# Attention mix on one core: one gate pass for all tokens, a landing rule for VectorE in the kernel's own scheduler, and a new table of its settings

## The chip, the core and the metric

The kernel runs on one core of a Trainium2 chip. The metric is the device time of one execution in microseconds, as a median of several runs. Times inside an execution come from one run taken with the hardware profiler; they count from its first instruction.

## What is computed

Two attentions over the same 2048 tokens of width 640, 32 heads of 20, mixed by a gate for each token:

```python
g = sigmoid((x * gate_w).sum(-1, keepdims=True))
# A: full softmax attention (every query with all 2048 keys)
scores = einsum("bhqd,bhkd->bhqk", q, k) * scale ; p = softmax(scores) ; o = p @ v ; a = o @ A_wo
# B: each query with 8 keys, 2 positions apart (idx = pos - 2 * w, masked below 0)
logits = einsum("bhsd,bhswd->bhsw", q, kg) * scale ; o = softmax(logits) @ vg ; b = o @ B_wo
return g * a + (1 - g) * b
```

## The kernel before, in words

The work of A sets the shape. Queries are taken in four chunks of 512 tokens and heads in eight groups of four: a *group* is one chunk with four heads, 32 groups in all (the last one is done in two halves of 256 tokens). The first 16 groups belong to chunks 0 and 1, the next eight to chunk 2, the last eight to chunk 3. Inside a group, a *unit* is one head with 128 keys: a matmul of contraction 32 that makes 128 x 512 scores in PSUM, then an exponential, then a product with the values that adds up in one bank, `obank`.

Scores go through two PSUM tiles, `score0` and `score1`, in turn. Each has three banks. A *tile* of work is two units or three: `qk(s)` (line 1690) issues its score matmuls (line 1708; row tiling, up to four heads at once), `exp(s)` (line 1728) lets ScalarE do the exponential of 1024 or 1536 columns into `ebuf` (line 1731), and `pv` (line 1743) issues the value products (line 1783; column tiling). Score tile s+2 needs the bank that exponential s reads.

Part of the units go to VectorE instead. Such a *ride* is one more score matmul in a tile, put into the third bank or into `side0`. VectorE turns it into an approximate exponential in integer arithmetic, by the scaled score put into the bits of a bf16 (line 1721, written as `uD`). Four rides make a quad; the quad's value product is done four times with weighted values (`vS`, made by GpSimd at line 893), and between these VectorE adds a constant to the bits (line 902). `wanted` and `next_tile` (lines 1562 and 1634) decide which units ride.

Everything else shares three *side banks*: `side0` and the third banks of the two score tiles. Python generators describe this work piece by piece: `gen_kd`, `gen_qd`, `gen_v` (the projections of A; a matmul group at line 606, then a VectorE copy out of the bank, lines 648, 721, 791), `gen_gate` (line 813), `gen_norm` (line 836: transpose of `obank`, reciprocal of the sums at line 844, scaling by `gA` and by the reciprocals on GpSimd at lines 850 and 858, transpose back at line 874, and transfers to `oTd`), `gen_bproj` and `gen_b` (all of B: copies at line 958, products at lines 974 and 1072, its own softmax and gate, with `tB` by a tanh at line 1048 and a reciprocal at line 1051), and `gen_fold` and `gen_prefold` (the output projections).

The order on each engine is made when the kernel is built. A scheduler written in the kernel keeps an estimated clock for each engine and appends instructions to five in-order lists. The loop over tiles lays `qk`, `exp` and `pv`; what room TensorE has left until the exponential ends is given to the generators (`run_side`, line 1343). A generator stops at a request such as `("pe", cost, ready)`, `("bank", need)`, `("act", ready)` or `("dve",)`, and `step` (line 1285) says whether it may go on now. For VectorE the test before was only how far that engine's own list had already been filled, and a ready time where the request named one:

```python
        elif req[0] == "dve":
            if not force and (sch.avail["dve"] > now + (req[1] if len(req) > 1 else DVE_AHEAD) or
                              len(req) > 2 and req[2] > max(now, sch.avail["dve"])):
                return False
```

`run_dve` (line 1351) fills VectorE's list in the same way ahead of a ride's conversion. `PLAN` is a table of 22 settings of this scheduler (slacks, priorities, how many units ride, when filler matmuls are laid), with new values from certain tiles on. Fillers (line 1804) are matmuls whose result nobody reads.

The gate in A's output: four matmuls of 32 columns for each of 5 parts of the width repeat the sum over all 128 partitions for one chunk of 512 tokens (line 606), a transpose (line 825) brings tokens to partitions, a tanh (line 828) and one VectorE operation (line 830) make `gA`. This is done once a chunk: for chunks 0 and 1 when group 1 begins, for chunk 2 and 3 shortly before their groups.

Of the kernel before, what the change touches and what calls it, by code (L numbers as in the profile page):

```python
# [10 lines left out]
ALU = mybir.AluOpType  # L11
# [9 lines left out]
CN = D // P  # L21
# [34 lines left out]
    0: ((0.3, 0.64), 0.32, 2.5, 2.5, 0.49, -1.3, -0.1, 11.8, 7.0, 7.2, 0.5, 0.47, 4.4, 4.0, -0.23, 0.75, 2, 0.0, 0.5, 4.0, 3.0, 1.0),  # L56
    10: ((0.28, 0.73), 0.32, 6.6, 2.5, 0.49, -0.79, -0.1, 11.8, 6.2, 5.51, 0.49, 0.47, 5.1, 4.63, -0.1, 0.75, 2, -1.5, 0.32, 4.0, 3.0, 1.0),
    30: ((0.28, 0.73), 0.32, 6.6, 2.5, 0.58, -0.79, -0.68, 11.8, 6.2, 5.51, 0.49, 0.47, 5.1, 4.63, -0.1, 0.72, 2, 0, 0.25, 4.0, 3.0, 1.0),
    40: ((0.28, 0.73), 0.32, 6.6, 2.5, 0.58, -0.79, -0.68, 11.8, 6.2, 5.51, 0.49, 0.47, 5.1, 4.63, 0.03, 0.74, 2, 0, 0.25, 4.0, 2.0, 0.0),
    50: ((0.28, 0.73), 0.32, 6.6, 2.5, 0.58, -0.79, -0.68, 12.65, 6.2, 5.51, 0.49, 0.47, 5.1, 4.63, -0.11, 0.74, 2, 0, 0.25, 4.0, 2.0, 0.0),  # L60
    60: ((0.28, 0.73), 0.37, 1.0, 2.5, 0.59, -0.79, -0.44, 11.8, 1.0, 6.14, 0.49, 0.47, 5.1, 4.63, -0.1, 0.72, 2, -3, 0.25, 4.0, 3.0, 1.0),
    70: ((0.28, 0.73), 0.37, 1.0, 2.5, 0.59, -0.79, -0.44, 11.8, 1.0, 6.14, 0.49, 0.52, 5.1, 4.63, -0.1, 0.72, 2, -3, 0.21, 4.0, 3.0, 1.0),
    80: ((0.28, 0.73), 0.32, 6.6, 5.5, 0.54, -0.74, -0.68, 12.65, 6.2, 6.19, 0.49, 0.47, 5.1, 5.79, -0.09, 0.66, 2, 0, 0.25, 4.0, 3.0, 0.0),
    90: ((0.28, 0.73), 0.13, 6.6, 5.5, 0.54, -0.74, -0.68, 12.65, 6.2, 6.19, 0.49, 0.47, 5.1, 5.79, -0.09, 0.66, 2, 0, 0.43, 4.0, 3.0, 0.0),
    100: ((0.28, 0.73), 0.13, 6.6, 6.6, 0.54, -0.74, -0.68, 12.65, 6.2, 6.19, 0.49, 0.47, 5.1, 5.79, -0.23, 0.63, 2, 0, 0.43, 4.0, 3.0, 0.0),
    110: ((0.28, 0.73), 0.36, 6.6, 6.6, 0.7, -0.74, -0.68, 12.65, 6.2, 6.19, 0.49, 0.47, 5.1, 5.79, -0.09, 0.66, 2, -3, 0.31, 4.0, 4.0, 0.0),
    120: ((0.28, 0.73), 0.36, 6.6, 6.6, 0.7, -0.48, -0.68, 12.65, 6.2, 6.19, 0.49, 0.47, 5.1, 5.65, -0.09, 0.66, 2, -3, 0.31, 4.0, 2.0, 0.0),
    140: ((0.28, 0.73), 0.36, 6.6, 6.6, 0.7, -0.48, -0.68, 12.87, 6.2, 5.74, 0.49, 0.47, 5.1, 5.65, -0.09, 0.66, 2, -3, 0.3, 4.0, 3.0, 0.0),
    150: ((0.28, 0.73), 0.45, 6.6, 2.5, 0.7, -0.48, -0.68, 12.87, 6.2, 5.74, 0.49, 0.47, 5.1, 6.51, -0.09, 0.72, 2, -3, 0.3, 4.0, 3.0, 0.0),
    160: ((0.28, 0.73), 0.5, 1.0, 2.5, 0.71, -0.48, -0.27, 12.87, 7.0, 5.74, 0.49, 0.47, 5.1, 7, -0.09, 0.72, 2, -3, 0.3, 4.0, 3.0, 0.0),  # L70
    170: ((0.24, 0.73), 0.46, 1.0, 6.6, 0.71, -0.89, 0.05, 12.87, 7.0, 5.74, 0.42, 0.47, 4.74, 7, -0.09, 0.72, 2, -3, 0.39, 4.0, 3.0, 0.0),
    180: ((0.24, 0.73), 0.46, 1.0, 6.6, 0.71, -0.89, 0.05, 12.87, 7.0, 5.74, 0.42, 0.47, 4.74, 7, -0.09, 0.72, 1, -3, 0.39, 4.0, 3.0, 0.0),
    190: ((0.28, 0.73), 0.42, 6.6, 6.6, 0.7, -0.74, -0.86, 12.65, 6.2, 6.19, 0.49, 0.38, 5.1, 5.79, -0.09, 0.66, 2, -3, 0.25, 4.0, 2.0, 0.0),
    200: ((0.28, 0.73), 0.42, 6.6, 6.6, 0.7, -0.61, -1.0, 10.61, 6.2, 7.31, 0.53, 0.38, 4.59, 5.79, 0.11, 0.66, 1, -3, 0.25, 4.0, 2.0, 0.0),
    220: ((0.28, 0.73), 0.31, 6.6, 6.6, 0.7, -0.61, -1.0, 9.36, 6.2, 7.31, 0.53, 0.38, 4.59, 5.79, 0.11, 0.66, 1, -3, 0.25, 4.0, 2.0, 0.0),
    230: ((0.25, 0.73), 0.33, 1.0, 1.0, 0.49, -0.79, -0.39, 11.8, 6.2, 5.77, 0.28, 0.47, 4.42, 4.63, -0.1, 0.73, 2, -3, 0.38, 4.0, 3.0, 0.0),
    240: ((0.25, 0.73), 0.33, 1.0, 1.0, 0.49, -0.79, -0.39, 11.8, 6.2, 5.77, 0.28, 0.45, 4.42, 4.63, -0.1, 0.73, 2, -3, 0.38, 4.0, 3.0, 0.0),
    250: ((0.28, 0.73), 0.5, 1.0, 5.5, 0.71, -0.48, -0.27, 12.87, 7.0, 5.74, 0.49, 0.65, 5.1, 7, -0.14, 0.72, 2, -3, 0.3, 4.0, 2.0, 0.0),
    260: ((0.28, 0.73), 0.5, 1.0, 5.5, 0.9, -0.48, -0.27, 12.87, 7.0, 5.74, 0.49, 0.65, 5.1, 7, -0.14, 0.72, 2, -3, 0.3, 4.0, 3.0, 0.0),
    270: ((0.28, 0.73), 0.5, 1.0, 1.0, 0.9, -0.48, -0.27, 12.87, 7.0, 6.71, 0.49, 0.65, 5.1, 7, -0.31, 0.72, 2, -3, 0.3, 4.0, 3.0, 0.0),  # L80
    280: ((0.28, 0.73), 0.59, 1.0, 1.0, 0.9, -0.48, -0.27, 12.87, 7.0, 6.71, 0.49, 0.69, 5.1, 7, -0.31, 0.72, 2, -3, 0.3, 4.0, 3.0, 0.0),
    290: ((0.28, 0.73), 0.31, 6.6, 2.5, 0.54, -0.74, -0.68, 11.34, 6.2, 8.37, 0.49, 0.47, 5.1, 5.79, -0.09, 0.74, 2, 0, 0.25, 4.0, 3.0, 0.0),
    300: ((0.28, 0.73), 0.31, 6.6, 2.5, 0.54, -0.74, -0.68, 11.34, 1.0, 8.37, 0.49, 0.32, 5.1, 5.79, -0.16, 0.74, 2, 0, 0.25, 4.0, 3.0, 0.0),
    310: ((0.28, 0.73), 0.31, 6.6, 2.5, 0.54, -0.74, -0.68, 11.34, 1.0, 8.37, 0.49, 0.1, 5.1, 5.79, -0.16, 0.74, 2, 0, 0.25, 4.0, 3.0, 0.0),
    320: ((0.38, 0.78), 0.22, 1.0, 6.6, 0.87, -0.76, -0.56, 12.65, 6.2, 6.19, 0.62, 0.38, 5.94, 6.4, -0.12, 0.73, 2, 0, 0.18, 4.0, 4.0, 0.0),
    330: ((0.38, 0.78), 0.22, 1.0, 6.6, 0.87, -0.76, -0.56, 12.65, 7.0, 6.19, 0.62, 0.38, 5.94, 5.7, -0.12, 0.73, 2, 1, 0.32, 4.0, 4.0, 0.0),
    340: ((0.38, 0.78), -0.02, 2.5, 6.6, 0.54, -0.76, -0.56, 12.65, 7.0, 6.19, 0.62, 0.38, 5.94, 5.7, 0.03, 0.73, 2, 1, 0.4, 4.0, 4.0, 0.0),
    350: ((0.28, 0.69), 0.29, 6.6, 6.6, 0.7, -0.48, -0.73, 12.65, 6.2, 4.72, 0.64, 0.47, 6.28, 6.04, -0.19, 0.66, 2, -3, 0.49, 4.0, 3.0, 0.0),
    360: ((0.28, 0.73), 0.32, 6.6, 2.5, 0.49, -0.79, -0.2, 11.8, 6.2, 7.02, 0.49, 0.47, 5.94, 5.65, -0.1, 0.73, 1, 0, 0.32, 4.0, 3.0, 1.0),
    370: ((0.28, 0.73), 0.32, 6.6, 2.5, 0.49, -0.79, -0.2, 11.8, 7.0, 7.91, 0.49, 0.47, 5.89, 5.65, -0.1, 0.67, 1, 0, 0.32, 4.0, 3.0, 1.0),  # L90
    390: ((0.28, 0.73), 0.21, 6.6, 5.5, 1.02, -0.48, -0.27, 12.69, 7.0, 5.74, 0.49, 0.65, 4.72, 7, -0.24, 0.75, 2, -3, 0.13, 4.0, 3.0, 1.0),
    400: ((0.28, 0.73), 0.21, 6.6, 1.0, 1.02, -0.48, -0.33, 12.76, 7.0, 5.74, 0.49, 0.77, 4.04, 7, -0.24, 0.75, 2, -3, 0.13, 4.0, 2.0, 1.0),
    410: ((0.28, 0.73), 0.21, 6.6, 1.0, 1.02, -0.48, -0.23, 12.76, 7.0, 5.74, 0.49, 0.77, 4.04, 7, -0.24, 0.75, 2, -3, 0.0, 4.0, 2.0, 1.0),
    420: ((0.28, 0.79), 0.21, 6.6, 5.5, 1.02, -0.48, -0.23, 12.76, 7.0, 5.39, 0.49, 0.77, 4.84, 7, -0.24, 0.7, 2, -3, 0.0, 4.0, 2.0, 1.0),
    430: ((0.28, 0.79), 0.21, 6.6, 5.5, 1.02, -0.48, -0.23, 9.83, 7.0, 5.39, 0.49, 0.77, 5.77, 7, -0.24, 0.73, 2, -3, 0.0, 4.0, 2.0, 1.0),
    450: ((0.28, 0.79), 0.21, 6.6, 5.5, 1.02, -0.48, -0.23, 9.83, 7.0, 5.39, 0.49, 0.77, 5.77, 7, -0.15, 0.73, 2, -3, 0.2, 4.0, 2.0, 1.0),
    470: ((0.28, 0.79), 0.21, 6.6, 5.5, 1.02, -0.67, -0.23, 9.83, 7.0, 5.39, 0.49, 0.77, 5.77, 7, -0.15, 0.73, 2, -3, 0.2, 4.0, 2.0, 1.0),
    490: ((0.28, 0.79), 0.21, 6.6, 1.0, 1.02, -0.89, -0.16, 9.83, 7.0, 5.39, 0.49, 0.58, 5.77, 7, -0.19, 0.73, 2, -3, 0.2, 4.0, 2.0, 1.0),
    500: ((0.28, 0.79), 0.21, 2.5, 1.0, 1.02, -0.89, -0.16, 9.55, 7.0, 5.39, 0.49, 0.58, 5.77, 7, -0.19, 0.73, 2, -3, 0.2, 4.0, 2.0, 1.0),
    510: ((0.28, 0.78), 0.32, 6.6, 6.6, 0.59, -0.74, -0.68, 12.65, 6.2, 6.19, 0.49, 0.38, 4.6, 5.79, -0.09, 0.68, 2, -3, 0.18, 4.0, 1.0, 1.0),  # L100
    520: ((0.33, 0.78), 0.32, 6.6, 6.6, 0.59, -0.95, -0.68, 12.65, 6.2, 6.19, 0.45, 0.38, 4.6, 5.79, -0.09, 0.68, 2, -3, 0.18, 4.0, 3.0, 1.0),
    530: ((0.28, 0.71), 0.21, 6.6, 5.5, 1.02, -0.48, -0.27, 12.69, 7.0, 5.74, 0.49, 0.71, 4.72, 6.53, -0.24, 0.75, 2, 0, 0.13, 4.0, 3.0, 1.0),
    540: ((0.28, 0.71), 0.21, 5.5, 1.0, 1.02, -0.48, -0.27, 12.37, 4.5, 5.74, 0.55, 0.71, 4.72, 6.53, -0.07, 0.75, 2, 0, 0.13, 4.0, 3.0, 1.0),
# [239 lines left out]
def _build(ctx, nc, A_x, A_wqkv, A_wo, B_wqkv, B_wo, gate_w, out):  # L343
# [469 lines left out]
    def gen_gate(qc):  # L813
        while qc > 1 and not all(done.get(("norm", POS[qc - 2, q])) for q in range(NQ)):
            yield ("cond",)
        while qc == 1 and not done.get(("gate", 0)) or qc > 1 and ulock[1]:
            yield ("cond",)
# [1163 lines left out]
```

## Time and profile before

| | before |
|---|---|
| runs | 802.10, 802.82, 803.96 us; median 802.82 |
| profiled execution | 802.35 us, span 800.5 us |
| ScalarE's first and last exponential start | 19.34 and 791.69 us |
| exponentials of 1024 / 1536 / 512 columns | 555 / 187 / 1 |
| rides converted by VectorE (line 1721) | 313 from score banks + 63 from `side0` |
| granted TensorE clock | 1.000 |

A line of the groups reads: source line, engine, operation, written tile, read tile and shapes, count, then busy time and mean duration in ns, then the engine's idle time ahead of these instructions and who ended it. A line of the waits reads: who waited, at which line, for whom; total us, how often, the longest. "issue" is idle time that the profile puts down to nothing. In the table by stretches every engine has its busy time and its count of instructions; then come the granted clock, the share of the DMA engines and GB/s. Engines overlap successive instructions, so durations of one engine may sum to more than the time that passes.

### The profile page before, as it was taken

What the parts mean: (1) busy time and instruction counts of PE and PEld (TensorE: products, weight loads), DVE (VectorE), ACT (ScalarE), POOL (GpSimd) and SP (SyncE); (2) the same over time, 40 slices, a digit from 0 to 9 for tenths busy, and PEclk for the clock granted to TensorE, in tenths of its full rate; (3) what the DMA queues carried; (4) which work ended last, traced back from release to release, by engine and by line L of the source; (5) the groups of instructions that cost most, each with busy time, mean ns of one, the idle gap of its engine ahead of it and who ended that gap; (6) DMA issues with size and microseconds to landing.
All of it is one profiled execution on the core that took longest, in us unless ns stands there. A gap on an engine that the chain in (4) does not pass through costs nothing.

```text
span 800.5 us, 29678 instructions
## 1 busy us (share of the span) xinstructions
PE 769.4 (96%) x12489; PEld 283.6 (35%) x12489; DVE 713.4 (89%) x1286; ACT 780.3 (97%) x777; POOL 144.8 (18%) x243
## 2 busy tenths in 40 slices
PE   8999989999999999999999999999999999899998
PEld 5333222233333343423343333333332333333243
DVE  6678889999888999898989999989999989899985
ACT  4999999999999999999999999999999999999996
POOL 5105111115411211111111011121011110211120
PEclk9999999999999999999999999999999999999999
DMA  9120101012012300300131130030220021103001
GB/s 304 53 50 7 29 16 34 23 36 70 22 35 49 67 20 19 77 12 22 35 90 22 28 85 14 22 91 23 57 48 10 17 64 44 32 6 73 10 11 35
DMA packets 59448, 35.27 MB, mean 44 GB/s; under 512 B 25252, under 2 KB 58116, under 8 KB 59316
## 3 DMA queue, kind: packets, MB, share of 16 engines
q1 hardware_dynamic: 59172, 33.21, 16.7%
q8 instruction: 99, 1.62, 0.8%
q14 instruction: 33, 0.27, 0.1%
q10 hardware_dynamic: 144, 0.16, 0.1%
HBM read 11.45 MB, written 2.62 MB: 18 GB/s over the span
## 4 chain that ended last, share of the span: by engine, by line
ACT 41%; PE 38%; issue 15%; DVE 4%; DMA 1%; SPq 0%; ACTq 0%
ACT ebuf L1731 41%; PE score L1708 13%; PE obank L1783 10%; PE side L606 7%; PE score L606 5%; DVE uD L1721 1%; DMA oB<-in_A_x_dram 1%; DVE uD L902 1%; PE score L990 0%; DVE kmd L651 0%; DVE qkvB L648 0%; ACT eB L1021 0%; PE score L1380 0%; PE obank L1804 0%; PE side L1804 0%
## 5 line engine op out<-in xcount | busy, mean ns | idle before, releaser
L1731 ACT ACTIVATE ebuf<-score 128x1024 bf16<-128x1024 f32 (+1 forms) x743 | 768.3, 1191 | 2.7 <-PE score L1708 1.7
L1708 PE MATMUL score<-qT,kT 32*128 32x512 bf16 (+1 forms) x2044 | 297.9, 378 | 22.4 <-ACT ebuf L1731 15.4
L1721 DVE TENSOR_SCALAR uD<-score 128x512 int16<-128x512 f32 x313 | 209.3, 681 | 25.6 <-PE score L1708 24.7
L902 DVE TENSOR_SCALAR uD<-uD 128x2048 int16<-128x2048 int16 x282 | 191.6, 698 | 6.3 <-PE obank L1783 5.7
L1708 PEld LDWEIGHTS score<-qT,kT 32*128 32x128 bf16 x2044 | 73.1, 91 | 265.5 <-ACT ebuf L1731 192.0
L1783 PE MATMUL obank<-ebuf,vA 128*21 128x512 bf16 (+1 forms) x1724 | 165.4, 380 | 0.6 <-DVE uD L902 0.4
L893 POOL TENSOR_TENSOR vS<-vA,vw 128x252 bf16<-128x252 bf16 x94 | 58.5, 622 | 455.0 <-DVE uD L902 239.4
L1783 PE MATMUL obank<-uD,vS 128*21 128x512 bf16 (+1 forms) x1128 | 98.2, 376 | 0.0
L606 PE MATMUL side<-xT,kvw 128*32 128x256 bf16 (+1 forms) x1960 | 82.6, 285 | 0.4 <-DVE uD L1721 0.3
L1783 PEld LDWEIGHTS obank<-ebuf,vA 128*21 128x21 bf16 x1724 | 41.2, 89 | 99.0 <-issue 77.0
L606 PEld LDWEIGHTS side<-xT,kvw 128*32 128x32 bf16 x1960 | 47.1, 96 | 26.4 <-issue 12.5
L974 DVE TENSOR_TENSOR stage<-qkvB 128x1280 bf16<-128x1280 bf16 x64 | 50.5, 813 | 0.0
L1072 DVE TENSOR_TENSOR stage<-stage,eB 128x1280 bf16<-128x1280 bf16 x64 | 50.3, 814 | 0.0
L858 POOL TENSOR_TENSOR oN<-oTt,rcp 128x256 bf16<-128x256 f32 (+1 forms) x62 | 40.5, 667 | 43.4 <-DVE uD L902 28.6
L1721 DVE TENSOR_SCALAR uD<-side 128x512 int16<-128x512 f32 x63 | 42.9, 680 | 2.5 <-PE side L1708 2.4
L606 PE MATMUL score<-xT,kvw 128*32 128x256 bf16 (+2 forms) x800 | 40.0, 296 | 0.7 <-ACT ebuf L1731 0.7
L1783 PE MATMUL obank<-uD,vA 128*21 128x512 bf16 (+1 forms) x388 | 33.6, 372 | 0.0
L958 DVE CAST qkvB<-side 128x512 bf16<-128x512 f32 (+1 forms) x52 | 30.7, 600 | 1.8 <-PE side L606 1.8
L1783 PEld LDWEIGHTS obank<-uD,vS 128*21 128x21 bf16 x1128 | 26.8, 91 | 11.4 <-issue 4.8
L850 POOL TENSOR_TENSOR rcp<-rcp,gA 128x16 f32<-128x16 f32 (+1 forms) x32 | 7.8, 245 | 111.0 <-DVE rcp L844 49.5
L840 DVE STREAM_TRANSPOSE oTt<-obank 128x512 f32<-128x512 f32 (+1 forms) x33 | 22.8, 692 | 3.6 <-PE obank L1783 3.4
L1708 PE MATMUL side<-qT,kT 32*128 32x512 bf16 (+1 forms) x68 | 24.2, 367 | 0.0
(215 smaller groups left out, 628.3 us busy)
## 6 DMA issues: line engine op xcount, KB each, us to landing
stage<-qkvB SPq DMA_DIRECT2D x128, 82.5 KB
stage<-in_B_wqkv_dram SPq DMA_DIRECT2D x1, 2400.0 KB
oTd<-oN SPq DMA_DIRECT2D x108, 20.0 KB
WqP<-in_A_wqkv_dram SPq DMA_DIRECT2D x13, 160.0 KB
qT<-dst SPq DMA_DIRECT2D x104, 20.0 KB
out_dram<-outsb SPq DMA_DIRECT2D x12, 160.0 KB
kvw<-in_A_wqkv_dram SPq DMA_DIRECT2D x2, 800.0 KB
qT<-qbnd SPq DMA_DIRECT2D x72, 1.0 KB
```

The source lines that it names most:

```text
L606: ins = e.matmul(o[j:k, :], l(j) if callable(l) else l[:, j:k], r, start=(first and i == 0), stop=(last and i == n - 1), skip_group_check= ...
L840: T("dve", 0.623 if W == 512 else 0.35, lambda e: e.transpose(oTt[:, 0:W], obank[:, 0:W]), reads=["obank"], writes=["oTt"])
L858: T(en, c2 if half < 0 else 0.56, lambda e: e.tensor_tensor(oo, ii, ib, ALU.mult), reads=["rcp", "oTt"], writes=[("oN0", h) for h in ((0, ...
L893: T("pool", 0.62, lambda e, t=t, kk=kk: e.tensor_tensor(vSd(d, t), _ap(vA, (kk * NQ + q) * 4 * DV, [[0, K - 1], [1, 4 * DV]]), _ap(vw, 0, ...
L902: T("dve", 0.066 + 0.1334 * n, lambda e, k=k: e.tensor_scalar(uD[u][:, 0:512 * n].bitcast(I16), uD[u][:, 0:512 * n].bitcast(I16), SHIFTS[k ...
L958: t = TB(dvc(n * TOK), lambda e, o=o, i=i: e.tensor_copy(o, i), reads=[("side", b)], writes=[key])
L974: TB(dvc(CN * TOK, 2), lambda e, w=w, ks=ks: e.tensor_tensor(prodB(w), qB[:, :, :], ks, ALU.mult), reads=["qB", "kB"], writes=[("prod", w) ...
L1072: TB(dvc(CN * TOK, 2), lambda e, o=o, vs=vs, ee=ee: e.tensor_tensor(o, vs, ee, ALU.mult), reads=["eB", ("prod", k)], writes=[("prod", k + ...
L1708: ins = e.matmul(o[:, n * t:n * t + n], kT[32 * j:32 * j + 32, q, kl[t] * P:(kl[t] + 1) * P], qT[min(g, LASTQ) % NQT][32 * j:32 * j + 32, ...
L1721: t = T("dve", 0.6, lambda e: e.tensor_scalar(uD[d % NU][:, 512 * i:512 * (i + 1)].bitcast(I16), side[y], UOFF, 0.0, op0=ALU.add, op1=ALU. ...
L1731: exps[s] = T("act", actc(512 * n), lambda e: e.activation(ebuf[s % NE][:, 0:512 * n], score[s % 2][:, 0:512 * n], ACTF.Exp, scale=LN2 / S ...
L1783: ins = e.matmul(obank[32 * j:32 * j + DV, 0:src.shape[-1]], v, src, start=(kb == 0), stop=(last and k >= len(lst) - 4), skip_group_check= ...
```

## The change

Three things are changed, and all else in the kernel stays as it is.

1. The gates of all 2048 tokens are made in one pass when group 1 begins. Each chunk of 512 tokens uses one column group of 32 partitions of the same bank, with one matmul instead of four for each fifth of the width. One transpose, one tanh and one VectorE operation follow. `gA` for a chunk is then filled by four small transfers from `g16` on SyncE's queue: for chunks 0 and 1 at once, for chunks 2 and 3 when the norms of chunk 0 and of chunk 1 are laid.
2. A VectorE request of a generator that holds side banks is held back until the matmuls in these banks should have landed, within `DRDY` us of the scheduler's present time. The reciprocal of B's gate waits in the same way for `tB`. The order only changes when the kernel is built; the instructions wait for the same things as before.
3. `PLAN` has new values in nearly all its 65 rows, starting at other tiles, and a 23rd setting, `DRDY`.

```diff
 PLAN = {
-    0: ((0.3, 0.64), 0.32, 2.5, 2.5, 0.49, -1.3, -0.1, 11.8, 7.0, 7.2, 0.5, 0.47, 4.4, 4.0, -0.23, 0.75, 2, 0.0, 0.5, 4.0, 3.0, 1.0),
...
+    0: ((0.3, 0.64), 0.32, 5.5, 2.5, 0.49, -1.3, -0.1, 11.8, 7.0, 7.22, 0.54, 0.47, 4.4, 4.0, 0.0, 0.75, 2, 0, 0.0, 4.0, 3.0, 1.0, 0.3),
...
-    def gen_gate(qc):
...
-        mms = [(side[b][:, :], gwrep(c), xT[:, c, qc * 512:(qc + 1) * 512]) for c in range(CN)]
-        yield from mm_group(b, mms, ["gwT"] + XT(qc), mmc(512))
...
-        T("dve", 0.1, lambda e: e.tensor_scalar(gA[qc % 2][:, :], g16[:, :], 0.5, 0.5, op0=ALU.mult, op1=ALU.add),
-          reads=["g16"], writes=[("gA", qc % 2)])
+    def gen_gate():
+        b = yield from bank()
+        for c in range(CN):
+            yield ("pe", mmc(512), sch.ready("gwT", *[k for qc in range(QCN) for k in XT(qc)]))
+
+            def fn(e, c=c, b=b):
+                for qc in range(QCN):
+                    ins = e.matmul(side[b][32 * qc:32 * qc + 32, :], _ap(gwT, c, [[0, 32]]), xT[:, c, qc * 512:(qc + 1) * 512],
+                                   start=(c == 0), stop=(c == CN - 1), skip_group_check=True)
+                return ins
...
+        T("dve", 0.1, lambda e: e.tensor_scalar(g16[:, :], g16[:, :], 0.5, 0.5, op0=ALU.mult, op1=ALU.add),
+          reads=["g16"], writes=["g16"])
+        done["gates"] = True
+        for qc in range(2):
+            gate_out(qc)
+
+    def gate_out(qc):
+        T("sp", 4.2, lambda e: [e.dma_start(gA[qc % 2][32 * i:32 * i + 32, :], g16[32 * qc:32 * qc + 32, :]) for i in range(4)],
+          reads=["g16"], writes=[("gA", qc % 2)], dma=True, nd=4)
+        done[("gate", qc)] = True
+
+    def gen_gate_out(qc):
+        while not all(done.get(("norm", POS[qc - 2, q])) for q in range(NQ)):
             yield ("cond",)
...
+        gate_out(qc)
...
-        yield ("dve",)
+        yield ("dve", DVE_AHEAD, sch.ready("tB"))
         t = TB(TQ * 7.5e-3, lambda e, b=b: e.reciprocal(rQ[:, :], side[b][:, 0:TQ]), reads=[("side", b), "tB"], writes=["rQ"])
...
+    DRDY = 2.0
+
+    def landing(ent):
+        return max([sch.ready(("side", b)) for b in range(NB) if bank_used[b] and bank_own[b] is ent], default=0.0)
+
...
         elif req[0] == "dve":
+            if not force and landing(ent) > max(now, sch.avail["dve"]) + DRDY:
+                return False
...
-                if ent[3][0] == "dve" and (len(ent[3]) < 3 or ent[3][2] <= max(sch.avail["dve"], limit - 0.7)):
+                if ent[3][0] == "dve" and (len(ent[3]) < 3 or ent[3][2] <= max(sch.avail["dve"], limit - 0.7)) and (
+                        landing(ent) <= max(sch.avail["dve"], limit - 0.7) + DRDY):
...
-                    add_gen(gen_gate(0), 1.5)
-                    add_gen(gen_gate(1), 1.6)
+                    add_gen(gen_gate(), 1.5)
...
-                    add_gen(gen_gate(g1 // NQ + 1), 4)
+                    add_gen(gen_gate_out(g1 // NQ + 1), 4)
```

In the new table `DRDY` lies between 0.26 and 1.1.

## The prediction

> **What bounds the kernel now.** I read the busy table of the page first, then the table by stretches, then ScalarE's groups with shapes kept apart, and last the starts of single instructions.
>
> ```profile
> span 800.5 us, 29678 instructions
> PE 769.4 (96%) x12489; PEld 283.6 (35%) x12489; DVE 713.4 (89%) x1286; ACT 780.3 (97%) x777; POOL 144.8 (18%) x243
> ```
>
> Three engines look full. The stretches say which one is the bound (columns: the stretch, its length, then busy time and count of PE, PEld, DVE, ACT, POOL):
>
> ```profile
> 0.00:20.00 20.00, 16.98 (x159) 10.33 (x160) 13.88 (x36) 9.58 (x14) 11.01 (x21) 1.00 0.93 304
> ...
> 400.00:500.00 100.00, 98.66 (x1768) 38.59 (x1768) 93.26 (x169) 99.88 (x102) 13.20 (x27) 1.00 0.20 48
> ...
> 780.00:801.00 21.00, 17.19 (x394) 8.12 (x382) 11.95 (x24) 12.65 (x13) 1.99 (x4) 0.98 0.10 34
> ```
>
> ScalarE is busy 99.88 of 100; it idles only in the head, before the first exponential at 19.34, and in the tail, after the last starts at 791.69. So the time is head + ScalarE's chain of exponentials + tail.
>
> ```profile
> L1731 ACT ACTIVATE ebuf<-score 128x1024 bf16<-128x1024 f32 x555 | 532.9, 1085 | 1.3 <-PE score L1708 0.7
> L1731 ACT ACTIVATE ebuf<-score 128x1536 bf16<-128x1536 f32 x187 | 270.3, 1508 | 1.4 <-PE score L1708 1.1
> ...
> L828 ACT ACTIVATE g<-qkvB 128x16 f32<-128x16 f32 x2 | 0.6, 296 | 0.0
> ```
>
> The durations overlap (555 x 1.085 + 187 x 1.508 is more than the span), so they don't price an instruction. The starts do: where nothing is awaited, a 1024-wide exponential is followed after 0.903 us, a 1536-wide one after 1.330, a 512-wide eB one after 0.477, a 64-wide tB after 0.103, a gate's tanh after 0.12. That prices ScalarE's work from 19.34 to 791.69 (772.35 us): 555 x 0.903 + 187 x 1.330 + 8 x 0.477 + 8 x 0.103 + 4 x 0.12 = 501.2 + 248.7 + 3.8 + 0.8 + 0.5 = 755.0. The other **17.3 us are waits for scores** that "busy" hides, some hundred of 0.05 to 0.5 us. Behind them is TensorE, in order: it reaches the score matmuls late, behind other matmuls, or waits for a bank that VectorE still reads:
>
> ```profile
> PEld score L1708 <- ACT ebuf L1731: 192.0, 487, 1.1
> PEld score L1708 <- issue: 43.6, 151, 0.4
> PEld score L1708 <- DVE uD L1721: 18.6, 45, 0.8
> ```
>
> The first line is healthy (TensorE ahead, waiting for ScalarE); the third (45 waits, 18.6 us) is what can starve it.
>
> **The change, part by part.** Everything but the gates is decided by the planner, so I counted the instructions as the two builds lay them out.
>
> *ScalarE.* Exponentials of 1024: 555 to 538; of 1536: 187 to 197. So 1667 score units of 512 where there were 1671: four go to VectorE's integer exponential (376 to 380 of those), and seven instructions fewer. By the starts: -17 x 0.903 + 10 x 1.330 = -15.35 + 13.30 = **-2.1 us**. Gates: four tanh become one, -3 x 0.12 = **-0.4 us**. Nothing hides ScalarE's work, so both count in full.
> The Trainium skill ("VectorE: DVE Perf Modes", section "The TRN2 errata") prices a ScalarE instruction from PSUM at 172 cycles plus one per element at 1.2 GHz; as an estimate from that page this is 0.997 and 1.423 us, and the first term would be -2.7. The trace disagrees: its starts leave a fixed part of 0.05 us, not 0.14, so the row decides.
>
> *TensorE.* The four gate passes were 80 matmuls of 512 (four column groups run together; 20 groups). Now 20 matmuls, one column group for each 512 tokens: 5 groups, -15 x 0.22 = -3.3 us of TensorE (0.22 is the spacing of groups in the trace). Four more units on VectorE cost 4 value products each instead of one. Without fillers, work other than scores comes to 363.9 us by 512 columns in 0.213, after 366.4. The planner lays 17 more filler groups (160 to 177). TensorE does not set the end by itself; 0 us.
>
> *VectorE.* Four more units: 4 x 0.60 (start to next start of L1721) + 3 more shift-adds x 0.60 (L902) = +4.2; three transposes fewer, -3 x 0.64; three small gate operations, -0.3: +2 us on an engine with 87 idle. Covered by that idle; 0 us. If the cover failed, 2.
>
> *The landing rule and the wait for tB* move VectorE instructions behind others; neither adds an instruction. Its target is seen in VectorE's groups (last column: idle before them and who ended it):
>
> ```profile
> L721 DVE TENSOR_SCALAR dst<-score 128x512 bf16<-128x512 f32 x11 | 7.5, 684 | 5.2 <-PE score L606 5.2
> L1051 DVE RECIPROCAL rQ<-score 128x64 f32<-128x64 f32 x5 | 2.8, 558 | 4.6 <-ACT tB L1048 4.6
> ```
>
> Such head-of-line waits (these two rows, L721 from side0 2.0, L648 from score 3.6, L1051 from side0 1.3, L958 from score 0.6 and side0 1.7) sum to some 19 us. A held instruction keeps its bank longer, though, and TensorE's next job in the bank waits. VectorE is not the bound; only what reaches ScalarE's 17.3 counts. L1721's line is 18.6 of the 62.2 us in which TensorE's score matmuls are late for something other than ScalarE (second and third line above), so 0.30 of 17.3 = 5.2 is its share of ScalarE's waits. From below all of it goes, -5.2; from above it doubles, +5.2. For the value I compared the builds, tile by tile: TensorE's work between two score tiles (0.213 a score tile, 0.21 for two changes of tiling, which the trace shows as 0.321 against 0.22 for a group beside a score tile, plus 0.213 for each other group) against the exponential of that tile. Before, 243 of 743 tiles overrun it, by 35.0 us in all, 19 by over 0.3; after, 240 of 736, by 32.5, 12 by over 0.3. In proportion the waits fall from 17.3 to 16.1; I take half of that, **-0.5**, since this count does not see VectorE.
>
> *Gates by DMA.* gA now comes by 16 small transfers. The nearest row, qT<-qbnd, takes 0.5 us to issue, so the first eight hold SP for 4 us. Behind them stand a WqP load and the transfers of qT for the fourth group, issued from 54.7 to 64.4 before; with 4 us more and a few to land they are there by about 72, and that group's first scores come at tile 74 (some 95 us). Its reader, the norm of group 0 on GpSimd, ran at 62.4; gates computed near 53 and landing near 60 are in time. The later eight (four for each half) have a whole group of about 25 us ahead. 0 us; uncovered, 4.
>
> *Tail.* After the last exponential, before:
>
> ```profile
> 792.36 0.40 PE L1783 MATMUL obank<-ebuf,vA 128*21 128x256 bf16 x8
> 792.59 0.28 PE L1783 MATMUL obank<-uD,vS 128*21 128x256 bf16 x4
> 792.70 0.28 PE L1783 MATMUL obank<-uD,xT 128*21 128x256 bf16 x4
> 792.99 1.26 PE L606 MATMUL side<-woBp,oB 128*32 128x512 bf16 x20
> ```
>
> There 8 uD matmuls stand behind the last ebuf ones; after, 24 do (+16 x 0.11/4 = +0.44), the last 8 behind a VectorE shift-add of 0.60 that 16 of the woBp matmuls (0.88) cover. Bounds 0 (the projections that follow are then shorter, and the chain over VectorE ends as late) and +1.0 (the shift-add uncovered); I take **+0.2**.
>
> **Sum.** -2.1 - 0.4 - 0.5 + 0.2 = -2.8, against the profiled execution's 802.35 (span 800.5): 799.55. The three timed runs' median, 802.82, is 0.47 above it; half of that in, I forecast **799.8 us**. About 0.2% (1.6 us) is what a measurement of this kernel can tell from no change: under 801.2 is faster, over 804.4 slower.
>
> **The rivals.**
> 1. *Forecast*: waits within 2 us of 16.8: 798 to 801.2. For it: ScalarE's work is counted, not guessed. 0.50.
> 2. *Waits fall far more*, because VectorE no longer blocks and releases score banks sooner: -5.2 for -0.5 gives 795.1. For it: the 18.6 us row. Against it: the landing rule acts on side banks, and that row is L1721, which the planner lays directly. Below 798: 0.15.
> 3. *Nothing to be seen*: waits grow by 1.5 to 4.5 us, as another order of the same work may, and swallow the gain: 802.5. This is also where the landing rule and the table do nothing and only the counts shift. Against it: by 50 us the waits lie evenly between 0.6 and 1.9, so another order should sum to much the same. 0.22.
> 4. *Slower, by TensorE in one place*: the new build lays tiles 300 to 400 (about 335 to 430 us) with hardly any 1536-wide exponentials (6 of 100). By the count above TensorE has 91.2 us of work there for ScalarE's 92.9, no filler at all; the tightest hundred before (350 to 450) had 97.0 for 100.1. Groups in the trace are spaced 0.216 to 0.223, not 0.213: 2 to 4% more on some 50 us, 1 to 2 us, and the slack of 1.7 is gone. From there each further 0.02 us a tile (one bank wait of 0.2 in ten tiles) is +2 us. It turns the whole slower when that place loses over 4.6 us; I price it at 5.2 (the doubled waits above): 805. 0.13.
>
> **Numbers.** Faster 0.50 + 0.15 = 0.65; same 0.22; slower 0.13. Range 796.0 to 804.5: it takes in the third case, both tail bounds and all but the last microsecond of the waits' bounds, and leaves out the whole of the deep gain and a TensorE place that loses over 4.7.
>
> **What would show it.** Right: exponentials 538 and 197; unstalled starts still 0.903 and 1.330; ScalarE's work between first and last exponential 752.6, its waits 15 to 19; head still 19.3; last exponential to end 8.8 to 9.2. Rival 2: waits under 12 and the L1721 line well below 18.6. Rival 4: ScalarE's share between 335 and 430 below 0.99, or many waits of 0.1 us there, behind TensorE without a gap. Wrong in another way: a granted clock below 1.00 in the body, SP's gate transfers followed by a wait of qT's scores, or a norm on GpSimd that waits for gA.

## The result, and the profile after

The changed kernel takes **804.99 us** (median of 7 runs, 804.91 to 805.48) where the kernel before takes 802.49 (7 runs, 802.10 to 803.96) on the same chip: a ratio of 1.0029, 95% interval 1.0019 to 1.0039. It is slower by some 2.5 us. The forecast was 799.8, the range ended at 804.5, and slower had a chance of 0.13.

The page of the changed kernel begins so:

```profile
span 803.1 us, 29718 instructions
PE 771.7 (96%) x12508; PEld 281.3 (35%) x12509; DVE 718.3 (89%) x1287; ACT 780.9 (97%) x767; POOL 145.8 (18%) x244
```

TensorE is busy for 2.3 us more, VectorE for 4.9. The same three stretches (columns as before):

```profile
0.00:20.00 20.00, 17.53 (x168) 11.08 (x169) 14.31 (x36) 10.00 (x14) 11.44 (x21) 1.00 0.94 305
400.00:500.00 100.00, 98.08 (x1745) 37.18 (x1741) 90.70 (x162) 99.92 (x103) 13.82 (x28) 1.00 0.21 49
780.00:803.00 23.00, 19.64 (x482) 9.52 (x470) 12.69 (x24) 14.52 (x13) 1.99 (x4) 0.96 0.10 33
```

The clock is full in the body, and ScalarE is still the bound (99.92 of 100). Its groups, shapes apart (the changed kernel's lines stand 12 to 20 further down: L1708, L1721, L1731, L1783, L902 and L1051 of before are now L1728, L1741, L1751, L1803, L914 and L1063):

```profile
L1751 ACT ACTIVATE ebuf<-score 128x1024 bf16<-128x1024 f32 x538 | 518.2, 1066 | 2.5 <-PE score L1728 1.5
L1751 ACT ACTIVATE ebuf<-score 128x1536 bf16<-128x1536 f32 x197 | 283.6, 1505 | 2.0 <-PE score L1728 0.8 <-PE side L1728 0.6
...
L830 ACT ACTIVATE g<-qkvB 128x16 f32<-128x16 f32 x1 | 0.2, 229 | 0.0
```

The counts are the forecast ones, and so are the unstalled starts (0.903 and 1.330). What changed is the remainder:

| us | before | after | difference |
|---|---|---|---|
| head, to the first exponential's start | 19.34 | 18.91 | -0.4 |
| ScalarE's work between first and last exponential, at the prediction's prices | 755.0 | 752.6 | -2.4 |
| the rest of that stretch: waits for scores | 17.4 | 22.2 | **+4.8** |
| last exponential's start to the end | 8.77 | 9.44 | +0.7 |
| span | 800.5 | 803.1 | +2.6 |

(Each difference is rounded by itself.)

The gain came as forecast, and waits took twice as much back. TensorE's waits ahead of its score matmuls, after:

```profile
PEld score L1728 <- ACT ebuf L1751: 184.2, 462, 1.2
...
PEld score L1728 <- issue: 52.1, 179, 0.6
...
PEld score L1728 <- DVE uD L1741: 14.6, 31, 0.8
```

The healthy first line lost 7.8 us. The line that I had taken for the one that starves TensorE (VectorE's conversion of a ride, 18.6 before) fell by 4.0. What grew is "issue", 43.6 to 52.1 us and 151 to 179 times: idle time for which the profile names no other engine, so TensorE's own work came under suspicion. VectorE's head-of-line waits, the target of the change, did shrink:

```profile
L721 DVE TENSOR_SCALAR dst<-score 128x512 bf16<-128x512 f32 x10 | 6.8, 682 | 1.3 <-PE score L606 1.1
...
L1063 DVE RECIPROCAL rQ<-side 128x64 f32<-128x64 f32 x6 | 3.3, 551 | 0.1
...
L1063 DVE RECIPROCAL rQ<-score 128x64 f32<-128x64 f32 x2 | 1.1, 550 | 0.0
```

The first stood at 5.2 us, the reciprocal at 4.6 from score banks and 1.3 from `side0`. The seven rows that the prediction had summed to 19 us now sum to 8.8. VectorE is not the bound, and the time does not show it.

### The profile page after: what moved, and what is told of

The parts are those of the page before. It is cut to its first block, busy times and chain, and to the rows that moved or that the text cites. A ratio compares the mean times of both kernels' runs of the same rounds, so it can differ in the third digit from the quotient of the medians.

```text
span 803.1 us, 29718 instructions
## 1 busy us (share of the span) xinstructions
PE 771.7 (96%) x12508; PEld 281.3 (35%) x12509; DVE 718.3 (89%) x1287; ACT 780.9 (97%) x767; POOL 145.8 (18%) x244
## 4 chain that ended last, share of the span: by engine, by line
PE 47%; ACT 31%; issue 12%; DVE 8%; DMA 1%; SPq 0%; POOL 0%; ACTq 0%; DVEq 0%; POOLq 0%
ACT ebuf L1751 30%; PE score L1728 16%; PE obank L1803 12%; PE side L606 8%; PE score L606 5%; DVE uD L1741 2%; DVE uD L914 2%; PE obank L1824 1%; DVE stage L986 1%; DMA oB<-in_A_x_dram 1%; PE score L1824 1%; PE side L1728 1%; PE side L1002 0%; PE side L1824 0%; DVE qkvB L970 0%
## 5 line engine op out<-in xcount | busy, mean ns | idle before, releaser
L1751 ACT ACTIVATE ebuf<-score 128x1024 bf16<-128x1024 f32 (+1 forms) x736 | 768.9, 1183 | 4.5 <-PE score L1728 2.3
L1728 PE MATMUL score<-qT,kT 32*128 32x512 bf16 (+1 forms) x2049 | 297.0, 378 | 19.8 <-ACT ebuf L1751 14.8
L1741 DVE TENSOR_SCALAR uD<-score 128x512 int16<-128x512 f32 x323 | 218.1, 683 | 34.4 <-PE score L1728 33.0
L914 DVE TENSOR_SCALAR uD<-uD 128x2048 int16<-128x2048 int16 x285 | 194.9, 697 | 3.5 <-PE obank L1803 2.9
L1728 PEld LDWEIGHTS score<-qT,kT 32*128 32x128 bf16 x2049 | 72.4, 91 | 265.6 <-ACT ebuf L1751 184.2
L1803 PE MATMUL obank<-ebuf,vA 128*21 128x512 bf16 (+1 forms) x1720 | 164.9, 380 | 0.6 <-DVE uD L914 0.4
L1803 PE MATMUL obank<-uD,vS 128*21 128x512 bf16 (+1 forms) x1140 | 100.7, 376 | 0.0
L606 PE MATMUL side<-xT,kvw 128*32 128x256 bf16 (+1 forms) x2150 | 90.1, 281 | 2.5 <-DVE qkvB L970 1.8
L1803 PEld LDWEIGHTS obank<-ebuf,vA 128*21 128x21 bf16 x1720 | 41.2, 88 | 101.1 <-issue 76.1
L606 PEld LDWEIGHTS side<-xT,kvw 128*32 128x32 bf16 x2150 | 51.1, 96 | 33.5 <-issue 14.0
L1741 DVE TENSOR_SCALAR uD<-side 128x512 int16<-128x512 f32 x57 | 39.1, 686 | 6.5 <-PE side L1728 5.9
L970 DVE CAST qkvB<-side 128x512 bf16<-128x512 f32 (+1 forms) x61 | 35.0, 585 | 3.9 <-PE side L606 3.9
L1803 PE MATMUL obank<-uD,vA 128*21 128x512 bf16 (+1 forms) x392 | 34.5, 372 | 0.0
L606 PE MATMUL score<-xT,kvw 128*32 128x256 bf16 (+1 forms) x610 | 32.9, 311 | 0.5 <-ACT ebuf L1751 0.5
L1803 PEld LDWEIGHTS obank<-uD,vS 128*21 128x21 bf16 x1140 | 27.1, 90 | 9.7 <-issue 2.9
L1824 PE MATMUL obank<-xT,zero 128*32 128x512 bf16 x316 | 25.3, 382 | 0.0
```

The source lines that it names most:

```text
L606: ins = e.matmul(o[j:k, :], l(j) if callable(l) else l[:, j:k], r, start=(first and i == 0), stop=(last and i == n - 1), skip_group_check= ...
L914: T("dve", 0.066 + 0.1334 * n, lambda e, k=k: e.tensor_scalar(uD[u][:, 0:512 * n].bitcast(I16), uD[u][:, 0:512 * n].bitcast(I16), SHIFTS[k ...
L970: t = TB(dvc(n * TOK), lambda e, o=o, i=i: e.tensor_copy(o, i), reads=[("side", b)], writes=[key])
L1728: ins = e.matmul(o[:, n * t:n * t + n], kT[32 * j:32 * j + 32, q, kl[t] * P:(kl[t] + 1) * P], qT[min(g, LASTQ) % NQT][32 * j:32 * j + 32, ...
L1741: t = T("dve", 0.6, lambda e: e.tensor_scalar(uD[d % NU][:, 512 * i:512 * (i + 1)].bitcast(I16), side[y], UOFF, 0.0, op0=ALU.add, op1=ALU. ...
L1751: exps[s] = T("act", actc(512 * n), lambda e: e.activation(ebuf[s % NE][:, 0:512 * n], score[s % 2][:, 0:512 * n], ACTF.Exp, scale=LN2 / S ...
```

## What the traces suggested: shared tiles

The changed kernel's timeline at one ride that goes into a side bank (columns: start, length, then engine, line, operation, tiles, count; in brackets the idle time ahead and who ended it):

```profile
93.35 0.39 PE L1728 MATMUL score<-qT,kT 32*128 32x512 bf16 x3 [0.44 <-ACT ebuf L1751]
...
93.59 0.37 PE L1728 MATMUL side<-qT,kT 32*128 32x512 bf16 x1
...
93.89 0.40 PE L1803 MATMUL obank<-ebuf,vA 128*21 128x512 bf16 x4
...
95.51 0.60 PE L1728 MATMUL score<-qT,kT 32*128 32x512 bf16 x3
...
96.15 1.02 ACT L1751 ACTIVATE ebuf<-score 128x1024 bf16<-128x1024 f32 x1 [0.17 <-PE score L1728]
```

The three score matmuls start together, the ride's 0.24 later (93.59), and the value products 0.54 after the first (93.89). Elsewhere the fourth matmul of such a tile starts 0.01 after the first, and the next work 0.32 after it. The heads tell the two kinds apart: this ride reads the same 32 partitions of `kT` and `qT` as one of the tile's own units. I call such a tile *shared*. The program says which tiles are: 47 of 743 before, 68 of 736 after. From the first matmul of a tile to TensorE's next work passed, at the median, 0.32 us in tiles without sharing (two, three or four units) and 0.53 to 0.54 in shared ones, in both traces. That is 0.21 us a tile, 9.9 us of TensorE before and 14.3 after.

The scheduler does not know it: `qk` charges 0.2155 us for every tile. `wanted` prefers a head that the tile does not use, but takes what is left of the quad. In tiles of two units and a ride, 39 of 361 were shared before and 48 of 348 after; in tiles of three and a ride, where one head alone is free, 8 of 15 and 20 of 32.

**Theory**: the 21 further shared tiles make the scores late. An exponential waits for the last matmul of its tile, since the scheduler signals a tile's score matmuls once, and that last one is the ride. In the changed trace the exponential of a shared tile waits 0.12 us on average, any other 0.02; before it is 0.10 and 0.02. **Rivals**: other work on TensorE (17 more filler groups), or thin margins of the new order that the shared tiles merely mark.

## Experiment 1: the same order with other numbers of shared tiles

The edit leaves every engine's list of instructions as it is. After the order is made, heads are exchanged within a group's four units of the same keys (a *four*), in the score matmul and in the value product alike (shortened):

```diff
+HEADS = {(3, 15): (0, 2, 1, 3), ...}
+HEAD = lambda g, kb, j: HEADS.get((g, kb), (0, 1, 2, 3))[j]
...
-                    ins = e.matmul(..., kT[32 * j:32 * j + 32, ...], qT[...][32 * j:32 * j + 32, ...], ...)
+                    h = HEAD(g, kb, j); ins = e.matmul(..., kT[32 * h:32 * h + 32, ...], qT[...][32 * h:32 * h + 32, ...], ...)
...
-            kl = kbs(g, kb)
+            kl, j = kbs(g, kb), HEAD(g, kb, j)
```

The changed kernel with none (69 fours exchanged):

> The instruction order of the changed kernel, engine by engine, with only the heads of some score units exchanged within their group of four keys' heads, so that no score tile holds two units of one head position (68 tiles do in the changed kernel, each 0.53 us instead of 0.32 us from its first matmul to the next piece of TensorE work). The output is the reference's. Theory (shared tiles): TensorE is freed of 68 x 0.21 = 14.3 us, and the exponentials' waits fall from 22.0 us by between 68 x 0.10 = 6.8 (the shared tiles' own excess over the others) and 68 x 0.21 = 14.3 (with the excess of the three tiles behind each): 791 to 798 us, 796 likeliest. Rival (thin margins or the extra fillers and side work cause the waits, the shared tiles are only where they show): waits stay above 20 us and the time within 1.5 us of 805.0.

The kernel before with none (48 fours):

> The same for the kernel before: 47 shared tiles to none, order unchanged, output the reference's. Theory: waits fall from 17.2 us by between 47 x 0.08 = 3.8 and 47 x 0.14 = 6.6 us: 796 to 799 us, 797.5 likeliest, and the order of the two kernels turns round: with no shared tiles on either side the changed one is faster by 1 to 3 us (head -0.4, exponentials' work -2.4, tail +0.6 us remain). Rival: 802.5 within 1.5 us, and the changed kernel still slower by about 2.5 us.

The changed kernel with 47 (13 fours):

> The changed kernel's order with as many shared tiles as the kernel before has: 47 instead of 68, by exchanging heads in 13 groups. Output the reference's. Theory: 21 tiles fewer at 0.10 to 0.21 us each: 800.6 to 802.9 us, about level with the kernel before (802.5) or up to 2 us under it. Rival: 805 within 1 us.

The kernel before with 68 (8 fours):

> The order of the kernel before with as many shared tiles as the changed kernel: 68 instead of 47, the 21 further ones put among tiles with a riding unit without regard to their margin. Output the reference's. Theory: +21 x 0.08 to 0.21 us: 804.2 to 807 us. Rival: 802.5 within 1 us.

And twice the changed kernel's number in both:

> The changed kernel's order with twice its shared tiles, 136 instead of 68, by exchanging heads in groups that ride. Output the reference's. Theory: each further one costs what the last ones gave, 0.10 to 0.18 us: 811.8 to 817.2 us. Rival (the first exchanges freed something that happened once, such as one late transfer): under 808 us.

> The order of the kernel before with 136 shared tiles instead of 47. Output the reference's. Theory: 89 x 0.08 to 0.18 us: 809 to 818 us, close to the changed kernel with the same number (that one has the thinner margins and 2.4 us less work for ScalarE). Rival: under 806 us.

| order of | shared tiles | median us | ratio to before, 95% | waits in the profile | tail |
|---|---|---|---|---|---|
| before | 0 | 799.16 | 0.9959 [0.9945, 0.9972] | 15.9 | 8.8 |
| before | 47 (as it is) | 802.49 | 1 | 17.4 | 8.8 |
| before | 68 | 805.88 | 1.0047 [1.0035, 1.0060] | 21.0 | 8.8 |
| before | 136 | 815.49 | 1.0161 [1.0139, 1.0182] | 30.6 | 8.8 |
| after | 0 | **795.76** | 0.9920 [0.9908, 0.9932] | 12.7 | 9.5 |
| after | 47 | 802.04 | 0.9996 [0.9988, 1.0005] | 19.0 | 9.6 |
| after | 68 (as it is) | 804.99 | 1.0029 [1.0019, 1.0039] | 22.2 | 9.4 |
| after | 136 | 817.06 | 1.0177 [1.0154, 1.0200] | 34.4 | 9.5 |

(Each ratio is to the kernel before on the same chip, from all runs, so it need not equal the quotient of the medians. The median of before is 802.49 us beside the changed kernel as it is, 802.16 beside the two with 136, and 802.08 beside the other four. The waits are of one execution.) Five of the six came out in the theory's range and the sixth, the order of before with none, 0.2 us above it; none came out where the rival put it. The exchange touches the value products too, but they start four at a time in all eight traces (819 fours in the order of before, 822 in that of after), so nothing changes there. In five of the six comparisons one shared tile costs 0.14 to 0.18 us of waits: (22.2 - 19.0)/21 = 0.15, (22.2 - 12.7)/68 = 0.14, (34.4 - 22.2)/68 = 0.18 in the order of after; (21.0 - 17.4)/21 = 0.17 and (30.6 - 17.4)/89 = 0.15 in that of before. The sixth, taking the 47 out of the order of before, gave (17.4 - 15.9)/47 = 0.03; more on it below.

With before's number the changed kernel is level with it, not faster: of the 4.8 us by which the waits rose, 3.2 (22.2 - 19.0) are the 21 further shared tiles' (2.6 us of time, by the ratios 1.0029 and 0.9996), and 1.6 (19.0 - 17.4) are still there at an equal number. With the longer tail these 1.6 use up what ScalarE's work gained. Where they come from was not tested; the same number of shared tiles may cost more in one order than in another. With none on either side the changed kernel is 3.4 us faster, against 1 to 3 expected.

The same place in the changed order without shared tiles:

```profile
92.60 0.39 PE L1728 MATMUL score<-qT,kT 32*128 32x512 bf16 x3 [0.44 <-ACT ebuf L1751]
...
92.61 0.39 PE L1728 MATMUL side<-qT,kT 32*128 32x512 bf16 x1
...
92.92 0.40 PE L1803 MATMUL obank<-ebuf,vA 128*21 128x512 bf16 x4
...
94.55 0.39 PE L1728 MATMUL score<-qT,kT 32*128 32x512 bf16 x3
```

The ride starts 0.01 after the others and the value products 0.32 after the first; the next score tile comes 1.95 us after this one instead of 2.16, takes 0.39 instead of 0.60, and ScalarE's chain no longer breaks there. In that kernel the waits for "issue" ahead of scores are down from 52.1 to 35.7:

```profile
PEld score L1728 <- issue: 35.7, 122, 0.4
```

The kernel before gave back less, 1.5 us of waits in its profile, and its runs spread from 797.4 to 800.6. The trace has one place for it, between 339 and 346 us:

```profile
ACT ebuf L1731 <- PE score L1708: 2.4, 3, 1.4
...
DVE stage L1072 <- DMA stage<-qkvB: 1.8, 1, 1.8
```

A transfer landed late, VectorE stood 1.8 us in front of it with the ride conversions behind, TensorE stood for 1.7 us, and three exponentials lost some 2.8 us, two of them after the granted clock had fallen to half for 3.41 us:

```profile
341.55:344.96 3.41, 3.15 (x41) 1.21 (x41) 3.34 (x7) 2.75 (x3) 0.00 (x0) 0.50 0.09 20
```

(The columns are those of the stretches: length, busy time of PE, PEld, DVE, ACT and POOL, then the granted clock, the DMA share and GB/s.) Without that 15.9 would be about 13.1, or 0.09 us for each of the 47. I did not pursue why this transfer is late there. The profile is of the slowest of this kernel's six executions (800.63 us); the two fastest, 797.38 and 797.89, lie at the 797.5 that I had called likeliest.

## Experiment 2: the fillers

The changed kernel lays 17 more filler groups. The edit cuts all 177 from 512 columns to 32 (shortened):

```diff
-  ins = e.matmul(o[32 * j:32 * j + 32, :], w..., xT[:, 0, 0:512], ...)
+  ins = e.matmul(o[32 * j:32 * j + 32, 0:32], w..., xT[:, 0, 0:32], ...)
```

> The changed kernel with its 177 groups of filling matmuls (line 1824, results unused, 17 groups more than before) cut from 512 columns to 32; order and output unchanged. Theory (shared tiles): fillers stand where TensorE had time to spare, so 0 to -2 us: 803 to 805. Rival (the 17 further fillers are what makes scores late): at least 17 x 0.15 = 2.5 us down, 802.5 or lower. If the fillers hold the clock up, the granted clock falls under 0.99 and the time rises.

> The changed kernel without shared tiles, and its fillers cut to 32 columns. Output the reference's. Theory: waits left at 12.7 us; some of the chains behind them pass a filler, so 0 to -2 us against 795.8: 793.8 to 795.8. Rival as for the fillers alone: 793 or lower.

Measured: 810.75 us (808.50 to 814.11; ratio 1.0101 [1.0076, 1.0127]) and 799.00 (795.57 to 802.10; 0.9950 [0.9926, 0.9974]). Both of my numbers for a harmless filler were wrong: by the medians, cutting them costs 6 us and 3 us. (The second is less certain: the interval of the kernel without shared tiles and with whole fillers, [0.9908, 0.9932], overlaps it slightly.) The condition that I had put beside the first held: the mean granted clock fell to 0.98. In the second it was 0.989. One stretch of the first (before the last two columns stands the granted clock, then the DMA share and GB/s):

```profile
101.00:121.50 20.50, 16.72 (x232) 4.92 (x228) 15.22 (x26) 18.92 (x18) 2.97 (x5) 0.84 0.04 11
```

and the same stretch of the changed kernel with its fillers:

```profile
101.00:121.50 20.50, 19.24 (x262) 5.31 (x250) 16.45 (x29) 20.20 (x19) 3.50 (x6) 1.00 0.04 11
```

The clock is at 0.84 and ScalarE is busy for 1.3 us less. TensorE's busy time over such a stretch does not decide the clock, though. In the second kernel, without shared tiles and with cut fillers too, TensorE is busy for less and the clock is full:

```profile
101.00:121.50 20.50, 16.28 (x267) 5.24 (x263) 17.61 (x30) 20.50 (x20) 3.00 (x5) 1.00 0.04 10
```

Shorter windows of the first show what its 0.84 is made of:

```profile
111.46:114.87 3.41, 2.10 (x39) 0.86 (x43) 2.79 (x5) 3.41 (x4) 0.61 (x1) 1.00 0.02 6
114.87:118.28 3.41, 2.83 (x31) 0.59 (x28) 1.79 (x3) 2.67 (x3) 0.00 (x0) 0.50 0.00 0
```

In this trace the granted clock is either full or half. Up to the last exponential it is half six times, for 3.41 us or two or three times that, and each time TensorE had been busy for only 1.85 to 2.33 of the 3.41 us before. That alone does not suffice: after 589.32 us it was busy for 2.05 of 3.42, and the clock stayed full.

Where the clock stood at 1.00 all the way, cut fillers save little: tiles 134 to 535 wait 11.9 us with whole fillers and 10.8 with cut ones, and without shared tiles the first 670 tiles wait 11.2 and 10.8. So all 177 groups together delay the scores by a microsecond or two, and the 17 further ones, if they are like the others, by a tenth of that. With the order kept, taking the fillers' columns away lowered the clock and cost more than that. The rival falls. The Trainium skill ("TensorE: Matmul & The Clock Gate", section "Why this matters for your kernels") asks for no idle gaps over some 3 us between bursts, since one such window brings the clock down. The trace disagrees on the gap: with cut fillers TensorE is nowhere idle for more than 0.95 us between matmuls, and the clock still fell. What exactly brings it down, no run here shows.

## Experiment 3: the code without the table, and the table without the code

> The code of the changed kernel (gates in one pass, the landing rule, the wait for the tanh half) with the table of before, its 23rd number set to 2.0 in each row. Output the reference's. The scheduler's own plan then ends at 925.9 us (before 793.7, changed 791.7), with 52 shared tiles; on the chip the two kernels end 8.7 and 13.2 us behind their plans, so 934 to 940 us. A rival by which the edits of the code help by themselves and the table only adds to it: under 802 us.

> The code of the kernel before with the new table, without its 23rd number. Output the reference's. The plan ends at 845.9 us, with 72 shared tiles; 8.7 to 13.2 us behind it on the chip: 854 to 860 us. A rival by which the table alone carries the effect: 803 to 807 us.

Measured, one run each: **939.07** and **862.53** us, beside 802.28 for the kernel before; waits of 148 and 75 us between first and last exponential. The first came where the scheduler's own plan put it, the second 2.5 us beyond. Neither part stands alone: each of the two tables fits its own code, and with the other's code it makes a far longer order. With the same code the old table gives 52 shared tiles and the new 68; with the old code the tables give 47 and 72. So in these four orders it is the **table** that brings most of the sharing (16 and 25 tiles more), and the code little (47 to 52, 72 to 68). The landing rule itself does nothing here: built with its threshold put out of reach (10^9), the changed program is the same, instruction for instruction, on every engine. By its clock no VectorE request comes up more than that threshold ahead of its matmuls. So the shorter waits of L721 are not its work; what the reciprocal's wait for `tB` does by itself was not tested on the chip.

## Why the prediction was wrong, point by point

- **ScalarE's work, -2.1 and -0.4**: right. Counts, prices and sum (752.6) are as forecast.
- **Waits for scores, -0.5**: this step failed. They rose by 4.8, near the upper bound of 5.2. I compared the two builds tile by tile with "0.213 a score tile", one price for every tile. The trace of before already held 47 tiles at 0.53, and the groups by line, whose means mix them, hide that. The 21 further shared tiles put 21 x 0.21 = 4.4 us of TensorE's time on top of an overrun that I had falling by 2.5, and experiment 1 puts 3.2 us of the rise down to them. The other 1.6 us, there at an equal number of shared tiles, I can't name. The size of that term was also tied to the wrong row: L1721's 18.6 us fell to 14.6 while the waits rose.
- **TensorE, 0 us, and "does not set the end by itself"**: wrong in the same way. Its chain between score tiles is what the exponentials wait for: 0.21 us more in it came through as 0.14 to 0.18 us in five of the six comparisons.
- **VectorE, 0**: right for the time. Its work grew by 4.9 us where I had 2, and went into its idle time; the 10 us by which the seven rows of head-of-line waits shrank bought nothing.
- **Gates by DMA, 0**: right for the time, as far as the trace shows, but a sign came that I had listed as "wrong in another way": the first norm on GpSimd waits for `gA`.

```profile
POOL rcp L862 <- DMA gA<-g: 11.3, 1, 11.3
```

The reciprocal ahead of it is done at 53.9 us, and GpSimd goes on at 59.2. The exponentials up to tile 80 wait 2.7 us in all, 2.3 before, so little came of it. Once, at 109.8 us, weight loads for scores stand 0.4 us for a transfer of `qT`.

- **Head**: I had it unchanged at 19.3; it was 18.9. It lies between 18.6 and 19.3 us in the eight kernels of experiment 1's table, 18.9 to 19.3 in the order of before and 18.6 to 19.1 in that of after, so of its -0.4 at most a part is the change's.
- **Tail, +0.2**: too small, +0.7. The 16 `woBp` matmuls cover the shift-add for TensorE all but some 0.1 us (their last group starts at 795.75, the products 0.33 after it, where groups of one kind are 0.22 apart):

```profile
795.10 1.04 PE L606 MATMUL side<-woBp,oB 128*32 128x512 bf16 x16
795.33 0.69 DVE L914 TENSOR_SCALAR uD<-uD 128x2048 int16<-128x2048 int16 x1 [0.38 <-PE obank L1803]
796.08 0.10 PEld L1803 LDWEIGHTS obank<-uD,vS 128*21 128x21 bf16 x4 [0.44 <-DVE uD L914]
```

But they stand ahead of the last products, which now start 2.5 us after the last exponential's start (1.0 before), and the last norm, which reads their sum, begins 1.5 us later. My term counted only the 16 further products and a possible wait for the shift-add; of the 1.5 us 0.7 are left at the end.

- **The rivals.** Rival 4 gave the right time, 805, for a wrong reason: between 335 and 430 us ScalarE is busy for 94.76 of 95 us, before for 94.64. Since "busy" hides waits, I also took the starts: 3.0 us of waits there, before 2.5, so its place lost half a microsecond. Rival 3 gave the right sign of the waits and, with +4.5 at most, nearly their size. Neither named sharing. Rival 2 (waits far lower, 795.1) is near what the same order does without shared tiles: 12.7 us of waits and 795.76.

The version without shared tiles beats both kernels: 795.76 us, 0.992 of before.

## What to carry to other kernels

Before a sum of "so many pieces at one price" is trusted, look at the spread of that price in the trace, piece by piece, and ask what sets the dear ones apart; a mean by line hides a second kind. Where an order is made by a scheduler's own clock, a new order is only as good as the costs in that clock, and what it does not price can grow unseen (here from 47 to 68). Such a fault is best tested with the order kept and only the operands exchanged.

## What the runs showed of the hardware

- Score matmuls of contraction 32 on different head positions mostly start 0.003 to 0.004 us apart and run together; a matmul on the same 32 partitions as one still running mostly starts 0.22 to 0.23 later, and TensorE's next work 0.21 later. The Trainium skill ("TensorE: Matmul & The Clock Gate", section "The mechanism" of its part on packing) has the first (about 4 ns); the trace agrees.
- With cut fillers the granted clock fell to half for 3.41 to 10.24 us at a time although TensorE was nowhere idle for more than 0.95 us. Over 20.5 us TensorE's busy time does not tell it: 16.72 us went with a clock of 0.84, 16.28 with 1.00. Matmuls whose results nobody reads were worth 3 to 6 us.
- An exponential was held by a matmul whose result it does not read, because the tile is signalled at its end: 0.12 us on average in shared tiles, 0.02 in others.
